# Routing attention and an ELU layer on one core: masks ahead of the scores in the ramp, weight conversion finished and weight sums made one block earlier

## The chip, the cores and the metric

The kernel runs on one core of a Trainium2 chip. The metric is the device time of one execution in microseconds (us). The kernel before the change takes 1039.99 us, the median of three runs (1039.98 to 1040.48). Engines carry the names of the profile: PE is the matrix engine, PEld its weight loads, DVE the vector engine, ACT the scalar engine, POOL the GpSimd engine, SP the queue that issues the transfers. "L252" is line 252 of the kernel before.

## What is computed

Attention in which a query sees only keys of its own cluster (the cluster is the nearest of 16 centroids, for queries and keys alike), and behind it a two-layer network with an ELU between the layers.

```python
# q, k, v: (4, 8, 768, 64) float32;  centroids: (8, 16, 64)
q_assign = argmax(q_n @ c_n.T);  k_assign = argmax(k_n @ c_n.T)
mask   = q_assign[:, :, :, None] == k_assign[:, :, None, :]
scores = where(mask, q @ k.T / 8, -1e9)
attn   = exp(scores - max) / sum(exp(scores - max))
x      = (attn @ v) -> (3072, 512)
# w_in: (512, 2048), w_out: (2048, 512): both arrive as float64
h = x @ w_in
g = where(h > 0, h, exp(min(h, 0)) - 1)
out = g @ w_out
```

The two weights are products of a float32 array and a float64 scalar, and so arrive as float64. [...]the kernel turns the 64-bit words into float32 by itself.

## The kernel before

The work is cut into 48 **blocks**: 4 batches, 3 thirds of 256 queries, 4 pairs of heads. Block n does the scores of block n and, one iteration later, the product with the values (`values(n)`). Seven blocks behind (`LAG = 7`) follows the network of a third, spread over four blocks: two blocks of `hidden` (the first layer) and two of `outer` (the second layer, seven half-size products in the manner of Strassen, which need sums and differences of the parts of `w_out`). The first seven blocks have no network beside them; they are called the ramp here. In the ramp the weights are converted, in 34 steps for 32 pieces of 128x512:

```python
def weight_steps():
    for n in range(len(pieces) + 2):
        if n > 1:          # finish piece n-2, then its buffer is free: ask for a later piece
            stt(ex, w[:, :, 1], 0x80000000, ex, bitwise_and, bitwise_or)     # DVE, L249
            stt(to, w[:, :, 0], 2.0**-32, to.bitcast(U32), mult, add)        # DVE, L252
            stt(to, to, 2.0**-20, ex.bitcast(F32), mult, mult)               # DVE, L255
            ask()                                                            # transfer on SP, L238
        if n < len(pieces):  # start piece n
            tensor_scalar(pieces[n][0], high, 0xFFFFF, 1 << 20, ...)         # DVE, L263
            tensor_scalar(e, high, 0x7FF00000, None, bitwise_and)            # DVE, L271
        if 0 <= n - 1 < len(pieces):
            activation(exps[n-1], exps[n-1], Relu, scale=8.0, bias=off)      # ACT, L274
        yield
def weigh(n): ...            # runs n of these steps
def sum_weights(half):       # e_, f_, g_, h_: quarters of w_out
    nc.vector.tensor_tensor(t1, f_, e_, op=subtract)     # DVE,  L304
    nc.gpsimd.tensor_tensor(f_, h_, f_, op=subtract)     # POOL, L305
    nc.vector.tensor_tensor(t2, h_, t1, op=subtract)     # DVE,  L306
    nc.vector.tensor_tensor(t4, g_, t2, op=subtract)     # DVE,  L307
```

The clusters become one-hot rows (`hot`), and a masked score is a second small matmul that adds `qm` times `hot`:

```python
def assign(b, j, at, size):          # j = 0: queries, in two halves of 384 (HS)
    ...                              # j = 1: keys, in batch 0 in three of 256 (QS)
    for e in range(2):
        if size == QS: nc.scalar.copy(h[64-at:128-at, 1, cols], h[at:at+64, 0, cols])    # ACT, L388
        else:   nc.vector.tensor_copy(h[64-at:128-at, 1, cols], h[at:at+64, 0, cols])    # DVE, L390
def masks(n):                        # qm of block n, two tiles in turn
    for e in range(2): nc.scalar.activation(qm[n][rows], hot[...], Identity, scale=m, ...)   # ACT, L401
def scores(n):                       # block 0 has a longer form
    for u in range(3):
        s = banks()                                  # one of three PSUM tiles of two banks
        ...                                          # PE: plain L425, mask L437
        nc.scalar.activation(p, s, Exp, scale=SCALE) # ACT, L448
        if n < LAG + 3: weigh(1)
def values(n):
    d = banks()
    ...                              # PE: p times v into o_bank L506; sums of p into d L495
    nc.scalar.activation(r, d, Ln)                    # ACT, L524
    nc.scalar.activation(e, d, Copy, accum_out=...)   # ACT, L525
    nc.scalar.activation(x, o_bank, Copy, scale=-1.0) # ACT, L526
    nc.scalar.activation(r, r, Exp, scale=-1.0)       # ACT, L527
    nc.vector.tensor_tensor(e, e, r, op=mult)         # DVE, L528
    nc.vector.scalar_tensor_tensor(r, e, -2.0, r, ...)# DVE, L529
    nc.gpsimd.tensor_tensor(x, x, r, op=mult)         # POOL, L532
def hidden(b, third, n):             # a quarter of the first layer
    h = banks(); ...                 # PE L547; ACT exp L557; POOL clip L558
    finish()                         # the elu of the quarter before: DVE L564, L566 or L568
def outer(b, third):                 # first .. fourth in one block, fifth .. seventh in the next
    first:  o_bank <- a, e_ ; ACT L608; DVE L609     second: f_bank <- b, g_ ; DVE L614, L615
    third_: o_bank <- c, f_ (written by L305)        fourth: f_bank <- d, t4 (written by L307); DVE L624
```

All products of `outer` have line L577. The order in which the blocks call all this:

```python
for n in range(len(blocks) + LAG):
    if n > 0: values(n - 1)
    ...                                        # loads of the next batch in blocks 5, 6, 9, 10; of v
    scores(n)
    masks(n + 1)
    if n >= LAG + 3: sums(n)
    turn(...)                                  # blocks 8 to 11: q and k of the next batch, DVE L319
    main = groups[n - LAG] if n >= LAG else []
    if n == LAG + 2:
        weigh(100)
        for half in range(2): sum_weights(half)
    for m, step in enumerate(main):            # hidden, or first .. fourth, or fifth .. seventh
        step()
        if n < LAG + 2: weigh(1)
```

Of the kernel before, what the change touches and what calls it, by code (L numbers as in the profile page):

```python
# [60 lines left out]
def main_path(ctx, tc, c, q, k, v, centroids, moe_w_in, moe_w_out, out):  # L61
# [8 lines left out]
    QS = S // NQ  # L70
# [38 lines left out]
    def load(name, i):  # L109
        b, pr = pairs[i]  # L110
        src = {"q": q, "k": k, "v": v}[name]
        if (name, i) in staged:
            t = first[:, ts(staged[name, i], 2 * NT * D)]
        elif name == "v":
            t = loads.tile([P, 2 * NT * D], F32, name="v_raw", tag="v", bufs=2)
        else:
            t = loads.tile([P, 2 * NT * D], F32, name=f"{name}_raw", tag="raw", bufs=4)
        if name == "v" or name == "q" and b == 0:
            t = t.rearrange("p (h t d) -> p h t d", h=2, t=NT)
            nc.sync.dma_start(  # L120
                t.rearrange("p h t d -> p h (t d)"),
                src[b, 2 * pr : 2 * pr + 2].rearrange("h (p t) d -> p h (t d)", t=NT),
            )
        elif b == 0:
            t = t.rearrange("p (t h d) -> p t h d", t=NT, h=2)
            for e in range(2):
                nc.sync.dma_start(
                    t[:, :, e], src[b, 2 * pr + e].rearrange("(p t) d -> p t d", t=NT)
                )
        else:  # L130

            for e in range(2):
                for g in range(2):
                    at = 64 * e + 32 * g
                    nc.sync.dma_start(
                        t[at : at + 32].rearrange("p (t a d) -> p t a d", t=NT, d=32),
                        src[b, 2 * pr + e, :, 32 * g : 32 * g + 32].rearrange(
                            "(a p t) d -> p t a d", a=4, t=NT
                        ),
                    )  # L140
        raw[name, i] = t
# [142 lines left out]
    def weigh(n):  # L284
        for _ in range(n):
            next(rest, None)
# [7 lines left out]
    def w_parts():  # L294
        e_, f_ = w_out[:, : FC // 2, :QS], w_out[:, : FC // 2, QS:]
        g_, h_ = w_out[:, FC // 2 :, :QS], w_out[:, FC // 2 :, QS:]
        return e_, f_, g_, h_

    def sum_weights(half):

        of = slice(half * FC // 4, (half + 1) * FC // 4)
        e_, f_, g_, h_ = (x[:, of] for x in w_parts())
        t1, t2, t4 = (w_sum[:, n, of] for n in range(3))
        nc.vector.tensor_tensor(t1, f_, e_, op=Alu.subtract)  # L304
        nc.gpsimd.tensor_tensor(f_, h_, f_, op=Alu.subtract)  # L305
        nc.vector.tensor_tensor(t2, h_, t1, op=Alu.subtract)  # L306
        nc.vector.tensor_tensor(t4, g_, t2, op=Alu.subtract)  # L307
# [38 lines left out]
    def similar(b, j, at, size):  # L346

        if at == 0:
            sim[b, j] = route.tile([P, S], F32, name="sim", tag="sim", bufs=1)
        ps = banks()[:, 0]  # L350
        cols = slice(at, at + size)
        for pr in range(NPR):
            nc.tensor.matmul(  # L353
                ps[32 * pr : 32 * pr + 32, :size],
                lhsT=cT[:, 32 * pr : 32 * pr + 32],
                rhs=T[b * NPR + pr, j][:, cols],
                start=True,
                stop=True,
            )
        return lambda: nc.vector.transpose(sim[b, j][:, cols], ps[:, :size])  # L360

    def assign(b, j, at, size):
        if at == 0:
            hot[b, j] = route.tile([P, 2, S], BF16, name="hot", tag=f"hot{j}", bufs=1 + j)
        cols = slice(at, at + size)
        n = size // NC
        s = sim[b, j][:, cols].rearrange("p (n c) -> p n c", c=NC)
        top = route.tile([P, HS // NC], F32, name="top", tag="top", bufs=1)[:, :n]
        oh = route.tile([P, HS], BF16, name="oh", tag="oh", bufs=1)[:, :size]
        nc.vector.tensor_reduce(top, s, axis=Axis.X, op=Alu.max)  # L370
        at = counted.setdefault(size, [])
        at.append(len(at) + (0 if size == HS else 4 * B - 2))
        at = at[-1]
        nc.vector.scalar_tensor_tensor(
            oh.rearrange("p (n c) -> p n c", c=NC),
            s,
            1.0,
            top.unsqueeze(2).to_broadcast([P, n, NC]),
            op0=Alu.mult,
            op1=Alu.is_equal,  # L380
            accum_out=count[:, at : at + 1],
        )
        h = hot[b, j]
        nc.vector.transpose(h[:, 0, cols], oh)  # L384
        for e in range(2):
            at = 64 * e
            if size == QS:
                nc.scalar.copy(h[64 - at : 128 - at, 1, cols], h[at : at + 64, 0, cols])  # L388
            else:
                nc.vector.tensor_copy(h[64 - at : 128 - at, 1, cols], h[at : at + 64, 0, cols])  # L390

    def side(pr, e):
        return int(pr // 2 != e)

    def masks(n):
        b, third, pr = blocks[n]
        qm[n] = route.tile([P, QS], BF16, name="qm", tag="qm", bufs=2)
        for e in range(2):
            rows = slice(64 * e, 64 * e + 64)
            m = big[rows, pr % 2 : pr % 2 + 1]  # L400
            nc.scalar.activation(  # L401
                qm[n][rows],
                hot[b, 0][rows, side(pr, e), ts(third, QS)],
                Act.Identity,
                scale=m,
                bias=minus[rows, pr % 2 : pr % 2 + 1],
            )


    LAG = 7  # L410
# [3 lines left out]
    blocks = [(b, third, pr) for b in range(B) for third in range(NQ) for pr in range(NPR)]  # L414
# [66 lines left out]
    def sums(n):  # L481
        to = osum[n] = work.tile([P, 2, 2 * QS], F32, name="psum", tag="psum", bufs=1)
        nc.vector.tensor_tensor(to, pu[n, 0], pu[n, 1], op=Alu.add)  # L483
        nc.vector.tensor_tensor(to, to, pu[n, 2], op=Alu.add)  # L484
        nc.vector.tensor_tensor(to[:, :, :QS], to[:, :, :QS], to[:, :, QS:], op=Alu.add)
# [174 lines left out]
    NB = NQ * NPR  # L660
# [3 lines left out]
    def load_v(n):  # L664
        b, third, pr = blocks[n]
        if n not in seen:
            seen.add(n)
            load("v", b * NPR + pr)
            raw["v", n] = raw.pop(("v", b * NPR + pr))
# [30 lines left out]
    for half in range(2):  # L700
        assign(0, 0, half * HS, HS)
    masks(0)

    for n in range(len(blocks) + LAG):
        b, at = n // NB, n % NB
        ahead = b + 1 < B
        if n <= len(blocks) and n > 0:
            values(n - 1)
        if ahead:
            for pr in {5: [0], 6: [1], 9: [2], 10: [3]}.get(at, []):  # L710
                load("q", (b + 1) * NPR + pr)
                load("k", (b + 1) * NPR + pr)
        if n + 1 < len(blocks):
            load_v(n + 1)
        if n < len(blocks):
            scores(n)
        if n + 1 < len(blocks) and at + 1 < NB:
            masks(n + 1)
        if n < len(blocks):
            if n >= LAG + 3:  # L720
                sums(n)
            if ahead and at in turns:
                for j in range(2):
                    turn((b + 1) * NPR + turns[at], j)
        beside = []
        if ahead and at + 1 == NB:
            beside.append(None)
            for j in range(2):
                beside.append(
                    lambda b=b, j=j: [similar(b + 1, j, half * HS, HS)() for half in range(2)]  # L730
                )
                beside.append(
                    lambda b=b, j=j: [assign(b + 1, j, half * HS, HS) for half in range(2)]
                )
            beside.append(lambda n=n: masks(n + 1))
        main = groups[n - LAG] if n >= LAG else []
        if n == LAG + 2:
            weigh(100)
            for half in range(2):
                sum_weights(half)  # L740
        done = 0
        for m, step in enumerate(main):
            step()
            upto = len(beside) * (m + 1) // len(main)
            for other in beside[done:upto]:
                if other:
                    other()
            done = upto
            if n < LAG + 2:
                weigh(1)  # L750
        for other in beside[done:]:
            if other:
                other()
        if n == len(blocks) + 1:
            verdict()

# [253 lines left out]
```

## Time and profile before

| | PE | PEld | DVE | ACT | POOL |
|---|---|---|---|---|---|
| busy, us of a span of 1038.0 | 1008.0 | 781.2 | 478.0 | 350.9 | 112.2 |
| share | 97% | 75% | 46% | 34% | 11% |

By stages, in us:

| stage | PE busy | DVE busy | ACT busy | granted PE clock |
|---|---|---|---|---|
| 0 to 26 | 17.39 | 19.28 | 14.26 | 1.00 |
| 26 to 52 | 24.02 | 17.39 | 17.21 | 0.93 |
| 52 to 78 | 24.22 | 23.13 | 19.43 | 1.00 |
| 78 to 104 | 24.37 | 23.97 | 17.73 | 1.00 |
| 104 to 130 | 25.80 | 21.45 | 13.11 | 1.00 |
| 130 to 156 | 21.69 | 25.62 | 9.02 | 0.96 |
| 156 to 182 | 24.11 | 13.44 | 5.79 | 0.78 |
| 312 to 1038 | 717.00 | 276.29 | 213.78 | 1.00 |

The table of stages is read as follows. In the last row PE is busy in 99 of 100 us. The stages with free PE time lie ahead of 182 us: block 0 ends near 34 us, the ramp near 98 us, and the first `outer` of the network begins at 144 us. The granted clock is the share of its full rate at which PE was allowed to run.

### The profile page before, as it was taken

The page shows a single profiled execution, that of the slowest core. Times are in us where ns is not written, and L with a number is a line of the kernel's source. Part 1 is how long each engine was busy: PE and PEld are TensorE (multiplying, and loading weights), DVE is VectorE, ACT ScalarE, POOL GpSimd, SP SyncE. Part 2 cuts the span into 40 slices and gives each one's busy share as a digit, 9 for nine tenths or more (in the row PEclk, how much of TensorE's full clock was granted, in tenths as well). Part 3 has the DMA queues.
Part 4 walks back from the last instruction along what each step waited for, and adds up shares of the span by engine and source line. Part 5 has one row for each costly group of instructions (what it writes and reads, how often), then busy time and mean ns, then how long its engine had stood idle before and what let it go on. Part 6 is the DMA issues. An engine that isn't in the chain of part 4 may idle for free.

```text
span 1038.0 us, 15007 instructions
## 1 busy us (share of the span) xinstructions
PE 1008.0 (97%) x6331; PEld 781.2 (75%) x6331; DVE 478.0 (46%) x775; ACT 350.9 (34%) x605; POOL 112.2 (11%) x129
## 2 busy tenths in 40 slices
PE   6999989999999999999999999999999999999997
PEld 4556766777777777778778778777877887788886
DVE  7689895463333334474234236365324423432121
ACT  5676532233332432333243243224223323421010
POOL 0001121110110110111011011011011011011010
PEclk9999997999999999999999999999999999999999
DMA  9738131100122113100122112201011010000000
GB/s 293 275 118 242 59 67 25 37 16 18 49 46 47 51 37 56 52 16 16 39 51 53 36 32 49 53 27 31 16 36 32 16 36 17 30 21 1 21 1 24
DMA packets 103962, 55.60 MB, mean 54 GB/s; under 512 B 83408, under 2 KB 96720, under 8 KB 103888
## 3 DMA queue, kind: packets, MB, share of 16 engines
q1 hardware_dynamic: 103888, 54.57, 19.2%
q8 instruction: 52, 0.85, 0.3%
q14 instruction: 22, 0.18, 0.0%
HBM read 48.27 MB, written 6.29 MB: 53 GB/s over the span
## 4 chain that ended last, share of the span: by engine, by line
PE 84%; DVE 10%; ACT 4%; issue 1%; POOL 0%; DMA 0%; DVEq 0%; ACTq 0%
PE banks L547 31%; PE f_bank L577 16%; PE o_bank L577 12%; PE o_bank L506 10%; PE banks L425 9%; PE banks L495 2%; PE banks L437 2%; DVE ex L249 1%; ACT p L448 1%; DVE w_in L252 1%; DVE w_out L252 1%; PE banks L353 1%; DVE w_in L255 1%; ACT e L525 1%; DVE ex L271 1%
## 5 line engine op out<-in xcount | busy, mean ns | idle before, releaser
L547 PE MATMUL banks<-xT,w_in 128*128 128x256 f32 x1536 | 338.4, 381 | 0.4 <-ACT p L448 0.2
L547 PEld LDWEIGHTS banks<-xT,w_in 128*128 128x128 f32 x1536 | 289.8, 190 | 48.0 <-issue 3.9
L425 PE MATMUL banks<-qT,kT 64*128 64x256 f32 x1152 | 167.2, 389 | 2.1 <-ACT e L525 0.8
L506 PE MATMUL o_bank<-p,v_raw 128*64 128x256 f32 x1152 | 144.6, 386 | 3.7 <-ACT p L448 3.7
L448 ACT ACTIVATE p<-banks 128x1024 f32<-128x1024 f32 x144 | 144.6, 1019 | 6.2 <-PE banks L437 4.2
L557 ACT ACTIVATE gT<-banks 128x1024 f32<-128x1024 f32 x48 | 49.1, 1023 | 279.1 <-PE banks L547 279.0
L564 DVE SCALAR_TENSOR_TENSOR gT<-gT,banks 128x1024 f32<-128x1024 f32 x48 | 58.4, 1217 | 156.4 <-POOL gT L558 156.3
L425 PEld LDWEIGHTS banks<-qT,kT 64*128 64x128 f32 x1152 | 87.7, 187 | 54.6 <-issue 11.1
L506 PEld LDWEIGHTS o_bank<-p,v_raw 128*64 128x64 f32 x1152 | 78.3, 137 | 57.3 <-issue 16.8
L524 ACT ACTIVATE r<-banks 128x256 f32<-128x256 f32 x48 | 18.4, 383 | 235.0 <-PE banks L495 234.9
L577 PE MATMUL o_bank<-w_out,gT 128*128 128x256 f32 x384 | 91.8, 393 | 6.2 <-POOL w_out L305 6.2
L528 DVE TENSOR_TENSOR e<-e,r 128x256 f32<-128x256 f32 x48 | 20.4, 425 | 161.0 <-ACT r L527 160.8
L577 PEld LDWEIGHTS o_bank<-w_out,gT 128*128 128x128 f32 x384 | 74.1, 196 | 20.6 <-POOL w_out L305 7.3
L558 POOL TENSOR_SCALAR gT<-gT 128x1024 f32<-128x1024 f32 x48 | 50.0, 1042 | 343.8 <-ACT gT L557 343.8
L577 PE MATMUL f_bank<-w_out,gT 128*128 128x256 f32 x384 | 86.8, 379 | 0.0
L532 POOL TENSOR_TENSOR xT<-xT,r 128x256 f32<-128x256 f32 x48 | 37.8, 788 | 448.4 <-DVE r L529 448.4
L437 PE MATMUL banks<-qm,hot 64*128 64x256 bf16 x576 | 81.3, 269 | 4.1 <-DVE hot L384 2.2
L577 PEld LDWEIGHTS f_bank<-w_out,gT 128*128 128x128 f32 x384 | 73.0, 190 | 9.9
L483 DVE TENSOR_TENSOR psum<-p 128x1024 f32<-128x1024 f32 x38 | 46.8, 1233 | 36.1 <-ACT p L448 36.1
L401 ACT ACTIVATE qm<-hot,minus,big 64x256 bf16<-64x256 bf16 x96 | 56.6, 590 | 1.1
L484 DVE TENSOR_TENSOR psum<-psum,p 128x1024 f32<-128x1024 f32 x38 | 46.6, 1226 | 5.9 <-ACT p L448 2.6
L577 PE MATMUL f_bank<-w_sum,g_sum 128*128 128x256 f32 x192 | 44.6, 386 | 0.6 <-DVE part L624 0.6
(111 smaller groups left out, 810.4 us busy)
## 6 DMA issues: line engine op xcount, KB each, us to landing
v_raw<-in_v_dram SPq DMA_DIRECT2D x48, 384.0 KB, 3.2
w_sum<-in_moe_w_out_dram SPq DMA_DIRECT2D x12, 512.0 KB, 4.4
out_dram<-o_sb SPq DMA_DIRECT2D x24, 256.0 KB, 2.1
q_raw<-in_q_dram SPq DMA_DIRECT2D x48, 96.0 KB, 3.2
k_raw<-in_k_dram SPq DMA_DIRECT2D x48, 96.0 KB, 2.9
w_sum<-in_moe_w_in_dram SPq DMA_DIRECT2D x8, 512.0 KB, 7.6
w_out<-in_moe_w_in_dram SPq DMA_DIRECT2D x8, 512.0 KB, 10.9
w_out<-in_moe_w_out_dram SPq DMA_DIRECT2D x4, 512.0 KB, 4.1
```

Source lines behind the costliest of these rows:

```text
L401: nc.scalar.activation(qm[n][rows], hot[b, 0][rows, side(pr, e), ts(third, QS)], Act.Identity, scale=m, bias=minus[rows, pr % 2 : pr % 2 + 1],
L425: nc.tensor.matmul(s[:, e, ts(kt % 2, QS)], lhsT=T[i, 1][rows, ts(kt, P)], rhs=T[i, 0][rows, cols], start=n > 0 or kt % 2 == 0, stop=False ...
L437: nc.tensor.matmul(s[:, e, ts(kt % 2, QS)], lhsT=hot[b, 1][rows, side(pr, e), ts(kt, P)], rhs=qm[n][rows], start=False, stop=True, skip_gr ...
L448: nc.scalar.activation(p, s, Act.Exp, scale=SCALE)
L483: nc.vector.tensor_tensor(to, pu[n, 0], pu[n, 1], op=Alu.add)
L484: nc.vector.tensor_tensor(to, to, pu[n, 2], op=Alu.add)
L506: nc.tensor.matmul(o_bank[64 * e : 64 * e + 64, :QS], lhsT=raw["v", n][:, e, kt], rhs=p[:, e, ts(m, QS)], start=(kt == 0), stop=(kt == NT ...
L547: nc.tensor.matmul(hf[:, f], lhsT=w_in[:, ch, ts(4 * n + f, P)], rhs=xT[b, third][:, ch], start=(ch == 0 and f % 2 == 0), stop=(ch == KC - 1),
L557: nc.scalar.activation(t, hf, Act.Exp)
L558: nc.gpsimd.tensor_scalar(t, t, 1.0, 0.0, op0=Alu.min, op1=Alu.max)
L564: nc.vector.scalar_tensor_tensor(t, t, -1.0, hf, op0=Alu.add, op1=Alu.max)
L577: nc.tensor.matmul(to[:, :QS], lhsT=left[:, f], rhs=right[:, f], start=(f == 0), stop=(f == FC // 2 - 1),)
```

## The change

Four things are moved, and no arithmetic is added or taken away. The copies of the queries' one-hot rows of batch 0 go from DVE to ACT. In blocks 1 to 9 the masks of the next block are issued ahead of the scores of this block, and so stand ahead of its exponentials in ACT's queue. Three conversion steps are run behind block 0, and in block 7 two steps follow each `hidden` instead of one. So all 34 steps are issued by the scores of block 8, and `sum_weights` runs at the end of block 8 instead of in block 9, ahead of the first products of `outer`. The aim is to use idle time of DVE in block 0, to shorten the wait between a block's last conversion step and its next one, and to have the sums of the weights ready when `outer` first wants them.

```diff
@@ assign
-            if size == QS:
+            if b == 0:
                 nc.scalar.copy(h[64 - at : 128 - at, 1, cols], h[at : at + 64, 0, cols])
@@ the loop over blocks
+        early = 0 < n < LAG + 3
+        more = n + 1 < len(blocks) and at + 1 < NB
+        if more and early:
+            masks(n + 1)
         if n < len(blocks):
             scores(n)
-        if n + 1 < len(blocks) and at + 1 < NB:
+        if more and not early:
             masks(n + 1)
+        if n == 0:
+            weigh(3)
...
-        if n == LAG + 2:
-            weigh(100)
-            for half in range(2):
-                sum_weights(half)
         done = 0
         for m, step in enumerate(main):
             step()
...
             if n < LAG + 2:
-                weigh(1)
+                weigh(2 if n == LAG else 1)
         for other in beside[done:]:
             if other:
                 other()
+        if n == LAG + 1:
+            weigh(100)
+            for half in range(2):
+                sum_weights(half)
```

## The prediction

> **What bounds the kernel now.** I read first the page's slices (the span in 40 equal parts of 26 us; digits are tenths of busy time, PEclk tenths of the full clock):
>
> ```profile
> PE   6999989999999999999999999999999999999997
> ...
> DVE  7689895463333334474234236365324423432121
> ...
> PEclk9999997999999999999999999999999999999999
> ```
>
> From the eighth slice (182 us) PE is full, so the time is the PE work plus what PE loses ahead of 182 us. DVE is nearly full in slices 3 to 6 only, and slice 7 has a low clock. Next the waits of DVE and of PE within the first 200 us (sum, times, longest):
>
> ```profile
> DVE e L528 <- ACT r L527: 26.3, 10, 6.7
> ...
> PE o_bank L577 <- POOL w_out L305: 6.2, 2, 4.3
> ...
> PE o_bank L506 <- ACT p L448: 3.7, 6, 0.7
> ```
>
> Two places lose time: the ramp, where PE waits a little in every block, and block 9, where PE waits for the sums of the weights. The chain of waits shows what paces a ramp block (start, us, what):
>
> ```profile
> 42.86 0.72 ACT ex L274
> 43.59 0.37 ACT qm L401
> ...
> 44.72 0.38 ACT r L524
> ...
> 46.20 0.44 DVE e L528
> ```
>
> The chain goes from a conversion on ACT (L274) through the two masks (L401) and the normaliser (L524 to L527) to DVE (L528), and from there through DVE's conversions. L528 begins at 46.20, 56.29, ... 96.65: a period of 10.08 us. In each DVE idles 0.77 us, and works 9.31.
>
> In DVE's timeline the end of block 0 shows a larger hole, behind the L271 that starts at 29.09 (the bracket is the idle time before, and what ended it):
>
> ```profile
> 36.20 0.43 DVE L528 TENSOR_TENSOR e<-e,r 128x256 f32<-128x256 f32 x1 [6.69 <-ACT r L527]
> ```
>
> and the timelines of DVE and PE in block 9 read
>
> ```profile
> 151.04 1.18 DVE L304 TENSOR_TENSOR w_sum<-w_out 128x1024 f32<-128x1024 f32 x1
> 152.25 1.22 DVE L306 TENSOR_TENSOR w_sum<-w_out,w_sum 128x1024 f32<-128x1024 f32 x1
> 153.51 3.25 DVE L307 TENSOR_TENSOR w_sum<-w_out,w_sum 128x1024 f32<-128x1024 f32 x1
> ```
>
> ```profile
> 144.24 3.72 PE L577 MATMUL o_bank<-w_out,gT 128*128 128x256 f32 x16
> 147.80 3.62 PE L577 MATMUL f_bank<-w_out,gT 128*128 128x256 f32 x16
> 155.73 3.78 PE L577 MATMUL o_bank<-w_out,gT 128*128 128x256 f32 x8 [4.31 <-POOL w_out L305]
> 161.40 3.78 PE L577 MATMUL o_bank<-w_out,gT 128*128 128x256 f32 x8 [1.89 <-POOL w_out L305]
> ```
>
> The third product stops twice for POOL, and its 8 records take as long as 16 did at 144.24: half the clock. The fourth, at 164.97, takes 4.90 us instead of 3.62.
>
> **What the Trainium skill says.** "TensorE: Matmul & The Clock Gate", section "What's actually happening": after an idle window of about 3.4 us PE falls to half rate, and needs about as long of busy time to come back. The trace agrees: after the idle 4.31 us the matmuls are half as fast, and are slow into the fourth product. The same page, section "Architectural detail: the array is 16× 32×32, not 1× 128×128": ACT and DVE are strict first-in first-out. So a mask issued after a conversion waits for it, as in the chain above. "SBUF — State Buffer", section "Who interferes with whom": DVE instructions with two SBUF inputs contend with POOL instructions that read SBUF. The trace agrees: L307 takes 3.25 us beside POOL's L305 (3.38), the same shape in L306 1.22. "Perfetto Trace Analysis", section "Optimizing Scalar/DVE Operations": work can go from a full DVE to ACT. In block 0, ACT idles 2.83 us ahead of its first key copy at 21.61.
>
> **The change part by part.**
>
> *Copies to ACT.* DVE loses two pairs of 64x384 copies, 0.55 and 0.44 us: about 1.0. ACT gains four; its own 64x384 copies (L342) take 0.96 a pair, so about 1.9 us more, into its idle 2.83. The first mask matmul (21.64) should come about 0.6 earlier and the last exponential of block 0 (27.69) about 1.0 earlier.
>
> *Three steps behind block 0.* From one L263 to the next (39.47 to 42.07) a step takes 2.60 us of DVE; three take 7.8. The hole of 6.69 plus the 1.0 saved is 7.7. So DVE becomes continuous here, and block 0's L528 stays at about 36.1. Gain at this point: nothing. These steps pay later, in block 9.
>
> *Masks ahead.* The two masks (43.49 to 44.70, 1.2 us) leave the stretch between the last conversion and L524. They then lie between L527 and the next exponential. New limits of a ramp block: DVE's work, 9.31. Or the loop DVE step, ACT conversion (0.7), third exponential (1.0), third part of the values on PE (1.8), L524 to L527 (1.5), L528/L529 and the next step (4.0): about 9.1 with the gaps. Or PE: values and row sums 12 groups of 0.433 (from one start to the next at full clock), 5.2, and scores 3.46 (34.60 to 38.06): 8.7. DVE is the longest. Six periods, L528 of block 0 to that of block 6, fall from 60.45 to 55.9: gain 4.6. The first exponential ends 2.1 us behind L528 instead of 0.9; the first `hidden` needs its PSUM tile and starts at L528 + 2.2 instead of + 1.46 (98.11 - 96.65). Net at the start of `hidden`: 3.9, at about 94.2.
>
> *Two steps per `hidden` in block 7.* Two more steps, 5.2 us, into a hole of 4.27 (before 118.99). With POOL's clips in the way L528 comes about 20.8 behind the start of `hidden`; before 20.88. Gain nothing, loss nothing.
>
> *Masks ahead in block 8.* Here one PSUM tile is held by the second `hidden`, whose ELU comes only in block 8. Before, PE's third score unit waited for the first exponential (0.3 us, 119.92) and the third `hidden` for the second (0.17 us, 121.44). Both are now pushed by 1.2 us of masks: loss 1.3.
>
> *Sums in block 8.* The last `hidden` ended at 135.46. ACT's exponential, POOL's clip and the ELU (2.1 + 1.9) end 4.1 us later; then `sum_weights` takes what it took before, 151.04 to 162.4, 11.3 us. So counted from the end of `hidden`, X: both L305 are done at X + 4.1 + 5.65 + 1.2 + 3.4 = X + 14.4, all sums at X + 15.4. PE wants `f_` (third product) at X + 15.8 and `t4` (fourth) at X + 19.3: the waits vanish, with 1.4 us to spare. DVE comes to L614, which frees f_bank for the fourth product, after L528/L529 (0.9), two transposes (1.8), L609 (1.2) and itself (0.4): X + 19.7 to 20. Loss 0.6. Before, 144.24 to 169.81 were 25.57 us for four products of 3.49: 11.6 lost. Gain 11.0.
>
> The sum: 3.9 - 1.3 + 11.0 = 13.6 us. All later PE work is full and moves up as it is: 1040.0 - 13.6 = 1026.4 us.
>
> **The rivals.**
>
> *The wait only moves.* If the sums on DVE start late (two contended L307, the steps of block 8, the transposes), the third product stops for L305 again. For: the slack is only 1.4 us, and DVE is nearly full from 130 to 156 us (25.62 of 26). Against: five of eight conversion steps of blocks 8 and 9 are gone from that stretch, 5 x 2.6 = 13 us. A wait of some 2 us without the half clock: 1029; long enough for the half clock: 1032 or more.
>
> *The masks take from the exponentials what they give to the normaliser.* PE takes up the values about 3.6 us after the scores began, and the first exponential then ends about when PE wants it. For: PE already waits for L448 0.7 us a block. Against: that wait is for the third exponential, which hangs on the conversion and not on the masks. If it happens, the ramp gains 0 to 1: 1030.
>
> *A transfer takes over.* The three steps behind block 0 put three weight transfers ahead of the next v transfer in SP's queue, which then leaves at about 36.5 instead of 34.28, and must land by 46.5. v took 3.2 us to landing in the median, 9.9 for the one at 26.88. Two us of wait once: 1028.4.
>
> *Better than the sum.* Block 0 ends with half clock (27.6 to 31.05, where 16 records took 3.4 us instead of 1.7). With shorter waits there the clock may stay up: 1.7 us more, 1024.7.
>
> **Range and chances.** The block 9 term is the surest, as it is read as a hole in PE; the ramp term depends on DVE having no new gaps (between 0.5 and 4.6 us), block 0 on the clock (up to 1.7 either way). I take 1022.5 to 1030.5. 2% would be 20.8 us, below 1019.2; all holes and half clocks I have named come to 11.6 + 4.6 + 1.7 = 17.9. So faster by over 2% gets 0.04, within 2% 0.94, slower by over 2% 0.02.
>
> **What would show it.** Right: L528 in the ramp every 9.3 us, with no idle time of DVE before it; DVE without a hole from 26 to 36 us; no wait for L305 and a full clock in the slice of block 9; four products from start to values in 14 to 15 us. Wrong in the ramp: a period near 10, with PE waiting for L448 at the first unit of the values. Wrong in block 8: no wait of PE for L448 ahead of the third `hidden`, which would add the 1.3 us. Wrong in block 9: PE waiting for L305 or L614 for more than 1 us. The prediction falls if PE after 170 us shows new holes, for it takes the rest as unchanged.

## The result, and the profile after

The changed kernel takes 1026.03 us (median of four runs, 1025.86 to 1026.78), against 1039.99 before (four runs by then, 1038.40 to 1040.48): a ratio of 0.987, with a 95% interval of 0.9853 to 0.9887. Predicted were 1026.4 us. The profiled spans are 1024.7 and 1038.0 us.

The page's slices of the changed kernel (25.6 us each, digits in tenths):

```profile
PE   6999999999999999999999999999999999999997
...
DVE  7999972753244244473334344375224324423131
...
PEclk9999999999999999999999999999999999999999
```

The dip of PE and of its clock in slices 6 and 7 is gone. DVE is now full from slice 2 to slice 5, so its hole at the end of block 0 is filled. The waits of DVE within the first 200 us (sum, times, longest) begin with

```profile
DVE e L528 <- ACT r L527: 10.7, 2, 6.4
```

Before these were ten waits with a sum of 26.3 us. Of the two that are left none lies in the ramp (they begin at 163.45 and 180.64). The waits of PE in the same time:

```profile
PE o_bank L506 <- ACT p L448: 1.9, 6, 0.8
...
PE banks L425 <- ACT p L448: 1.2, 1, 1.2
...
PE f_bank L577 <- DVE o_sb L614: 0.2, 1, 0.2
```

The wait for POOL's L305 is no longer among them. A new one, L425 for L448, is 1.2 us long. In the chain of waits of one ramp block (start, us, what)

```profile
46.08 0.37 DVE e L528
...
54.98 0.34 DVE ex L271
55.32 0.36 DVE e L528
```

everything between these lines is DVE: ACT has left the chain, and each L528 follows the last conversion instruction without a pause. But ACT is only just ahead. In its timeline of the same block

```profile
53.89 0.39 ACT L524 ACTIVATE r<-banks 128x256 f32<-128x256 f32 x1 [0.41 <-PE banks L495]
...
54.79 0.42 ACT L527 ACTIVATE r<-r 128x256 f32<-128x256 f32 x1
```

the normaliser (L524 to L527), which waits for PE, ends at 55.21, and DVE's timeline has L528 start at 55.25. So DVE's own work and the loop from DVE through ACT's conversion, the third exponential, PE's values and the normaliser back to L528 end within 0.04 us of each other. This trace does not tell which of the two sets the period of 9.23 us.

In DVE's timeline there is no pause at the end of block 0 either:

```profile
36.52 0.42 DVE L271 TENSOR_SCALAR ex<-w_sum 128x512 uint32<-128x512 uint32 x1
36.85 0.42 DVE L528 TENSOR_TENSOR e<-e,r 128x256 f32<-128x256 f32 x1
```

The sums of the weights in DVE's timeline, and the first four products of `outer` in PE's:

```profile
137.30 1.22 DVE L304 TENSOR_TENSOR w_sum<-w_out 128x1024 f32<-128x1024 f32 x1
138.55 1.22 DVE L306 TENSOR_TENSOR w_sum<-w_out,w_sum 128x1024 f32<-128x1024 f32 x1
139.81 3.26 DVE L307 TENSOR_TENSOR w_sum<-w_out,w_sum 128x1024 f32<-128x1024 f32 x1
```

```profile
141.94 3.72 PE L577 MATMUL o_bank<-w_out,gT 128*128 128x256 f32 x16
145.49 3.62 PE L577 MATMUL f_bank<-w_out,gT 128*128 128x256 f32 x16
148.95 3.62 PE L577 MATMUL o_bank<-w_out,gT 128*128 128x256 f32 x16
152.81 3.72 PE L577 MATMUL f_bank<-w_sum,gT 128*128 128x256 f32 x16 [0.24 <-DVE o_sb L614]
```

The sums cost DVE what they cost before, but they start 4.6 us ahead of the first product instead of 6.8 behind it. All four products run at full clock. What the change costs stands in PE's timeline of block 8:

```profile
117.48 0.70 PE L425 MATMUL banks<-qT,kT 64*128 64x256 f32 x4 [1.25 <-ACT p L448]
...
119.14 14.08 PE L547 MATMUL banks<-xT,w_in 128*128 128x256 f32 x64 [0.30 <-ACT p L448]
```

The third score unit and the third `hidden` wait for exponentials that now stand behind the masks.

Behind this the two programs move alike: from the first product of the first second half of `outer` (178.59 before, 165.25 after) to the last product of all (1029.18, 1015.82) it is 850.59 and 850.57 us. So the gain lies ahead of that point, and five numbers of each trace tell where. They are used for all runs below: the L528 of block 0, the ramp's period (mean of six), the start of the first `hidden`, from there to the third `hidden`, and from the first product of `outer` to the fifth, which holds the hole of block 9.

| run | L528, block 0 | period | first hidden | to third hidden | first to fifth product | time, us |
|---|---|---|---|---|---|---|
| before | 36.20 | 10.08 | 98.11 | 23.33 | 34.35 | 1039.99 |
| after | 36.85 | 9.23 | 94.47 | 24.67 | 23.31 | 1026.03 |
| e1, masks late | 36.88 | 10.08 | 98.79 | 23.66 | 23.32 | 1029.89 |
| e2, masks to 7 | 36.48 | 9.23 | 94.11 | 23.31 | 23.31 | 1025.38 |
| e3, copies on DVE | 37.71 | 9.29 | 95.66 | 24.66 | 23.31 | 1027.88 |
| e4, sums in block 9 | 36.94 | 9.23 | 94.59 | 24.66 | 26.01 | 1029.62 |
| e5, no steps in block 0 | 34.67 | 9.26 | 92.47 | 24.66 | 25.86 | 1027.60 |
| e6, no sign | 36.29 | 9.02 | 92.64 | 24.65 | 23.31 | 1024.16 |
| e7, masks only | 36.56 | 9.24 | 94.22 | 24.67 | 32.07 | 1034.89 |
| e8, two steps | 35.84 | 9.23 | 93.47 | 23.31 | 23.32 | 1023.42 |
| e9, sums only | 37.26 | 10.08 | 99.19 | 23.66 | 23.31 | 1030.60 |
| e10, after again | 36.22 | 9.24 | 93.88 | 24.66 | 23.31 | 1026.85 |
| e11, masks to 6, two steps | 35.11 | 9.24 | 92.45 | 23.33 | 23.32 | 1023.32 |
| e12, PE filled | 33.64 | 9.35 | 91.64 | 23.33 | 23.31 | 1023.08 |

The times are medians of four runs each. The same changed kernel took 1026.03 and 1026.85 us on two occasions, and its L528 of block 0 came at 36.85 and 36.22. The runs were made in three groups (e1 to e4, e5 to e8, e9 to e12), each on another chip, where the kernel before took 1039.68, 1039.83 and 1039.51 us. So a difference below 1 us between times of different groups is not read as an effect; the stages are, though each stage is from one trace.

### The profile page after: what moved, and what is told of

It reads as the page before. It is cut to its first block, busy times and chain, and to the rows that moved or that the text cites. A ratio compares the mean times of both kernels' runs of the same rounds, so it can differ in the third digit from the quotient of the medians.

```text
span 1024.7 us, 15010 instructions
## 1 busy us (share of the span) xinstructions
PE 1001.1 (98%) x6331; PEld 778.4 (76%) x6331; DVE 474.8 (46%) x771; ACT 354.1 (35%) x609; POOL 112.5 (11%) x129
## 4 chain that ended last, share of the span: by engine, by line
PE 81%; DVE 12%; ACT 3%; issue 2%; DMA 1%; POOL 0%; SPq 0%; DVEq 0%; POOLq 0%; ACTq 0%
PE banks L547 30%; PE f_bank L577 16%; PE o_bank L577 12%; PE o_bank L506 10%; PE banks L425 9%; PE banks L437 2%; PE banks L495 2%; DVE ex L249 2%; DVE w_in L252 1%; DVE w_in L255 1%; DVE w_out L252 1%; ACT p L448 1%; DVE ex L271 1%; PE banks L353 1%; DVE w_out L255 1%
## 5 line engine op out<-in xcount | busy, mean ns | idle before, releaser
L425 PE MATMUL banks<-qT,kT 64*128 64x256 f32 x1152 | 166.0, 388 | 3.3 <-ACT p L448 1.2
L448 ACT ACTIVATE p<-banks 128x1024 f32<-128x1024 f32 x144 | 144.5, 1020 | 6.4 <-PE banks L437 4.2
L425 PEld LDWEIGHTS banks<-qT,kT 64*128 64x128 f32 x1152 | 88.0, 187 | 53.0 <-PE o_bank L506 10.0
L524 ACT ACTIVATE r<-banks 128x256 f32<-128x256 f32 x48 | 18.4, 384 | 232.9 <-PE banks L495 232.9
L577 PE MATMUL o_bank<-w_out,gT 128*128 128x256 f32 x384 | 87.8, 382 | 0.0
L528 DVE TENSOR_TENSOR e<-e,r 128x256 f32<-128x256 f32 x48 | 20.4, 424 | 145.4 <-ACT r L527 145.2
L532 POOL TENSOR_TENSOR xT<-xT,r 128x256 f32<-128x256 f32 x48 | 37.4, 779 | 435.5 <-DVE r L529 380.8
L483 DVE TENSOR_TENSOR psum<-p 128x1024 f32<-128x1024 f32 x38 | 46.6, 1226 | 36.1 <-ACT p L448 36.1
```

Of the source, the lines that this page charges most:

```text
L425: nc.tensor.matmul(s[:, e, ts(kt % 2, QS)], lhsT=T[i, 1][rows, ts(kt, P)], rhs=T[i, 0][rows, cols], start=n > 0 or kt % 2 == 0, stop=False ...
L448: nc.scalar.activation(p, s, Act.Exp, scale=SCALE)
L577: nc.tensor.matmul(to[:, :QS], lhsT=left[:, f], rhs=right[:, f], start=(f == 0), stop=(f == FC // 2 - 1),)
```

## The experiments

**e1: masks behind the scores.** The changed kernel with

```diff
-        early = 0 < n < LAG + 3
+        early = False
```

> The changed kernel with the masks behind the scores again, in all blocks. My theory: the masks' 1.2 us go back into the stretch between the last conversion on ACT and the normaliser, so L528 in the ramp comes every 10.0 to 10.1 us instead of 9.23, with DVE idle 0.8 us before each: +5.1. The first hidden then starts 1.46 instead of 2.24 us behind L528: -0.8; block 8 loses its waits for the exponentials: -1.3. Sum +3.0, 1029.0 us. Rival: the ramp is paced by DVE's work alone and the gain came from the steps moved ahead; then the period stays 9.23 and the time is 1024.7 to 1026 us.

Measured 1029.89 us, where 1029.0 was expected. The period is 10.08 again, to the hundredth that of before, although the steps are moved and the copies are on ACT. So it is the order of the masks that makes the difference between 10.08 and 9.23, and not the moved steps: the rival is out. The third `hidden` comes 1.0 us sooner behind the first, where 1.3 was expected.

**e2: masks early in blocks 1 to 7.**

```diff
-        early = 0 < n < LAG + 3
+        early = 0 < n < LAG + 1
```

> The changed kernel, with the masks ahead of the scores in blocks 1 to 7 only, not in 8 and 9. My theory: the 1.25 us that PE's third score unit of block 8 waits for the first exponential are due to the masks of block 9 standing ahead of it; without them that wait falls to about 0.3 and the third hidden starts 23.3 instead of 24.67 us behind the first: 1024.7 us. Rival: the wait comes from the conversions between the exponentials on ACT; then nothing changes, 1026.0 us.

Measured 1025.38 us, between the theory and the rival, so the time alone does not decide. The trace does: from the first `hidden` to the third it is 23.31 us instead of 24.67, the expected 1.35. The wait of 1.25 us of the third score unit is no longer there. The masks of block 9 are what kept it waiting, not the conversions, which stand between the exponentials here too.

**e3: copies on DVE again.**

```diff
-            if b == 0:
+            if size == QS:
                 nc.scalar.copy(h[64 - at : 128 - at, 1, cols], h[at : at + 64, 0, cols])
```

> The changed kernel with the queries' one-hot copies of batch 0 on DVE again. My theory: DVE works without a hole from block 0's first finished piece to the end of the ramp, so whatever delays that start delays all: the first conversion on ACT (25.60) comes 0.8 to 1.0 us later, and so does L528 of block 0: 1026.8 to 1027.0 us. Rival: the copies lie beside other work; no change, 1026.0 us.

Measured 1027.88 us, a little above the theory. L528 of block 0 comes at 37.71, 0.86 us later than in the changed kernel's first trace and 1.49 later than in its second; the first conversion on ACT starts at 26.25 instead of 25.60. The copies are on the path, as expected. The exact size stays between 0.9 and 1.5 us, as L528 of the changed kernel itself differs by 0.63 between its two traces. The longer mean period, 9.29, is one block: there L528 (56.41) waits 0.23 us for ACT's L527, so the loop through ACT and PE can end last.

**e4: sums in block 9.** The `weigh(100)` and the `sum_weights` go back behind the scores and transposes of block 9; the steps stay where the change put them.

```diff
+        if n == LAG + 2:
+            weigh(100)
+            for half in range(2):
+                sum_weights(half)
         done = 0
...
-        if n == LAG + 1:
-            weigh(100)
-            for half in range(2):
-                sum_weights(half)
```

> The changed kernel with the sums of the weights back in block 9, all conversion still done by block 8. My theory: most of the 11 us of block 9 came from the conversion being through; the sums then start about 142.7, behind L528 and the transposes; the third product waits about 2.4 us for the second L305 and the fourth starts about 2.9 us later than now, with no half clock: 1028.9 us. Rival: the place of the sums is what counts; then the waits of before return with the half clock, +11: 1037 us.

Measured 1029.62 us. In PE's timeline the third product is split once:

```profile
149.06 1.89 PE L577 MATMUL o_bank<-w_out,gT 128*128 128x256 f32 x8
153.07 1.99 PE L577 MATMUL o_bank<-w_out,gT 128*128 128x256 f32 x8 [2.12 <-POOL w_out L305]
```

It waits 2.12 us and goes on at full clock; with L614 it is 2.70 us in all (26.01 against 23.31), 2.9 expected. So with the conversion through, 8.3 of the 11 us of block 9 are there already, and the place of the sums adds 2.7. The sums begin 0.64 us behind the first product here (142.69 and 142.05), and 6.80 behind it in the kernel before.

**e5: no steps behind block 0.**

```diff
-        if n == 0:
-            weigh(3)
```

> The changed kernel without the three conversion steps behind block 0; they then fall to the last hidden of block 8. My theory: block 0's L528 waits for ACT and not for DVE and comes 1.3 us earlier, and the ramp with it: -1.3. In block 8 three more steps lie on DVE ahead of the sums, which start about 2 us later; the third product still finds its parts, but L614 comes about 2 us later and the fourth product waits: +1.9. Sum +0.6: 1026.7 us. Rival: the three steps are what keeps the sums off PE's path; without them the third product waits again: 1029 us or more.

Measured 1027.60 us (1027.31 to 1030.52), where 1026.7 was expected. The bill is as expected in kind. Block 0's L528 waits for ACT, and comes at 34.67, 1.6 to 2.2 us earlier. In block 8 the last three steps lie ahead of the sums, and PE's timeline has

```profile
153.35 3.72 PE L577 MATMUL f_bank<-w_sum,gT 128*128 128x256 f32 x16 [2.80 <-DVE o_sb L614]
```

a wait for L614 of 2.80 instead of 0.24 us, and none for L305. So the three steps cost 1.6 to 2.2 us in block 0 and give 2.55 in block 9 (25.86 against 23.31): they are worth little.

**e6: no sign.** The changed kernel leaving out L249, so that the weights have no sign and the output is another; all else is the same work.

```diff
-                nc.vector.scalar_tensor_tensor(
-                    ex, w[:, :, 1], 0x80000000, ex, op0=Alu.bitwise_and, op1=Alu.bitwise_or
-                )
```

> The changed kernel, leaving out one of the five DVE instructions of each conversion step, L249, which puts the sign in (so the weights lose their signs). My theory: DVE's 9.23 us of work pace the ramp; with 3 x 0.60 us less PE becomes the limit, at 8.7 to 8.8 us a block: 6 x 0.45 = 2.7, and block 0's L528 1.3 earlier: 1022 us. Rival: ACT's chain of conversion, exponential and normaliser paces the ramp; then only block 0 gains, 1024.7 us.

Measured 1024.16 us, a miss against the 1022 of my theory. The trace says why (lines have numbers three lower here). In DVE's timeline

```profile
54.33 0.42 DVE L525 TENSOR_TENSOR e<-e,r 128x256 f32<-128x256 f32 x1 [1.46 <-ACT r L524]
```

DVE idles 1.46 us a block, so it is not the bound here. The period falls only to 9.02 us. PE's timeline shows it with scores from 43.77, values from 47.46 behind a wait of 0.16 us for the first exponential, and the next scores at 52.79: PE is the limit at 9.02, of which 8.86 are its own work, and not at the 8.7 that I had taken from starts of groups without the change-overs. The gain is 6 x 0.21 = 1.3 us in place of 2.7. In block 0 the half clock lasted longer in this run (a mean clock of 0.50 from 28 to 32 us, 0.61 in the changed kernel's first trace), and L528 came at 36.29. The run does not show whether DVE's work or the loop through ACT and PE held the 9.23: without L249 DVE has three instructions less to do in a block, and the loop is one instruction of 0.60 us shorter too.

**e7: masks only.** The kernel before with the masks ahead of the scores in blocks 1 to 9, as in the change, and nothing else of it.

```diff
+        early = 0 < n < LAG + 3
+        more = n + 1 < len(blocks) and at + 1 < NB
+        if more and early:
+            masks(n + 1)
         if n < len(blocks):
             scores(n)
-        if n + 1 < len(blocks) and at + 1 < NB:
+        if more and not early:
             masks(n + 1)
```

> The kernel before, with the masks ahead of the scores in blocks 1 to 9 as the only change. My theory: the ramp's period falls to 9.3 us, -4.9 over six blocks; the first hidden starts 0.75 later behind L528; block 8 loses 1.3; block 9 keeps its waits for L305: in all -2.8, 1037.2 us. Rival: without the other parts the masks bring nothing, 1040 us.

Measured 1034.89 us, 2.3 better than expected. The stages up to block 9 are as expected: period 9.24, first product at 141.69, 2.55 us earlier than before. The rest is in block 9, in PE's timeline:

```profile
152.53 1.99 PE L577 MATMUL o_bank<-w_out,gT 128*128 128x256 f32 x8 [3.67 <-POOL w_out L305]
158.20 3.38 PE L577 MATMUL o_bank<-w_out,gT 128*128 128x256 f32 x8 [3.68 <-POOL w_out L305]
161.42 3.62 PE L577 MATMUL f_bank<-w_sum,gT 128*128 128x256 f32 x16
```

PE waits longer than before (7.35 us instead of 6.20), but after the first wait the clock is still full, and only the second half of the product is slow. From the first product to the fifth it is 2.28 us less: the waits are 1.15 us longer, but fewer records ran at half clock (the fourth product takes 3.62 us, before 4.90). That is nearly all of the 2.3.

**e8: two steps behind block 0, masks to block 7.** In the changed kernel:

```diff
-        early = 0 < n < LAG + 3
+        early = 0 < n < LAG + 1
...
-            weigh(3)
+            weigh(2)
```

> The changed kernel with two steps behind block 0 instead of three, and the masks ahead in blocks 1 to 7 only. My theory: -1.3 from block 8 (as in the run with masks to 7), and with two steps DVE is done before the normaliser of block 0, whose L528 comes 1.3 us earlier; the one step that is left falls into a hole of DVE in block 8: 1023.4 us. Rival: what block 0 gives is lost to the sums in block 8: 1024.7 us.

Measured 1023.42 us, as expected in sum. The block 8 part is there (23.31 us to the third `hidden`), and the wait for L614 stays 0.25 us. L528 of block 0 waits for ACT again and comes at 35.84, which is 1.01 and 0.38 us earlier than in the changed kernel's two traces, not 1.3; this trace is of the slowest of the four runs (1024.41). So that the sum fits so closely is in part luck.

**e9: steps and sums only.** The kernel before with the three steps behind block 0, two per `hidden` in block 7, and the sums at the end of block 8.

```diff
+        if n == 0:
+            weigh(3)
...
-        if n == LAG + 2:
...
-                weigh(1)
+                weigh(2 if n == LAG else 1)
...
+        if n == LAG + 1:
```

> The kernel before with only the steps moved (three behind block 0, two per hidden in block 7) and the sums in block 8; masks and copies as before. My theory: block 9 is whole, 14.5 instead of 25.6 us for the four products, -11.0; the ramp keeps its 10.08 us; block 0's L528 comes 1.3 us later, as DVE has the copies and three more steps there: in all -9.7, 1030.2 us. Rival: the block 9 gain needs the faster ramp too; then 1033 us or more.

Measured 1030.60 us, 8.9 less than the 1039.51 of before in the same group. The block 9 hole is gone whole (23.31) with the ramp at 10.08, so this gain does not need the faster ramp; e7 shows that the ramp's does not need the sums. -8.9 here and -4.9 in e7 make 13.8, and the change gave 14.0, but that is no proof that the two add up: the 2.3 us that e7 gained in block 9 stand in both, and the copies on ACT (0.9 to 1.5 us by e3) in neither.

**e10: the changed kernel again**, unchanged.

> The changed kernel once more, unchanged, beside the three others on the same chip: 1026.0 us, within 0.7.

Measured 1026.85 us (1026.12 to 1027.37), just outside the 1025.3 to 1026.7 that were expected.

**e11: masks to block 6, two steps.**

```diff
-        early = 0 < n < LAG + 3
+        early = 0 < n < LAG
...
-            weigh(3)
+            weigh(2)
```

> The changed kernel with two steps behind block 0 and the masks ahead in blocks 1 to 6 only. Masks of block 7 no longer stand ahead of the exponential that frees the PSUM tile of the first hidden: 0.3 us less than with masks to 7 and two steps (1023.4): 1023.1 us. Rival: the first hidden waits for POOL's last xT and not for the tile; then 1023.4 us.

Measured 1023.32 us, against 1023.42 of e8 in another group: the times can't tell 0.3 us. The traces can. The first `hidden` starts 1.92 us behind L528 (92.45 and 90.53) instead of 2.24, without a wait, while POOL's last xT was still at work in POOL's timeline:

```profile
91.69 1.08 POOL L532 TENSOR_TENSOR xT<-xT,r 128x256 f32<-128x256 f32 x1 [8.24 <-DVE r L529]
```

It ends at 92.77, behind that start. So the wait that the changed kernel's trace puts down to POOL's L532 (0.25 us at 94.47) was for the PSUM tile, and the exponential that frees it ended at 94.33.

**e12: PE filled in block 0.** The kernel of e11, with six more matmuls into `f_bank` that nobody reads:

```diff
                 for m in range(2):
                     mask(units[u], 2 * u + m)
+                for _ in range(2 * (u + 1) if u < 2 else 0):
+                    nc.tensor.matmul(f_bank[:, :QS], lhsT=T[i, 1][0:64, ts(0, P)],
+                                     rhs=T[i, 0][0:64, cols], start=True, stop=True)
                 exponentials(units[u], u)
```

> The kernel of the run with masks to 6 and two steps, with six more small matmuls in block 0 whose results nobody reads, in the gaps where PE waits for masks and exponentials. Theory that the half clock behind block 0 (16 to 22 records at half speed) comes from those gaps: the clock stays full, the values of block 0 end 1.8 to 2.2 us earlier, L528 with them, 1021.3 us. Rival: the clock follows something else or has its own beat; then nothing, or up to 0.5 us more, 1023.1 to 1023.6 us.

Measured 1023.08 us (1021.89 to 1023.47) against 1023.32 (1022.58 to 1024.00) of e11: no difference that these runs resolve. But the first half of the theory holds. The stages of e11 and of this run, with PE's busy time first (behind the length) and the granted clock behind POOL's:

```profile
24.00:28.00 4.00, 1.99 (x13) 0.86 (x12) 2.90 (x8) 3.60 (x6) 0.00 (x0) 0.78 1.03 413
28.00:32.00 4.00, 4.00 (x32) 2.43 (x30) 3.77 (x9) 3.02 (x6) 0.00 (x0) 0.79 1.03 411
```

```profile
24.00:28.00 4.00, 3.46 (x26) 2.25 (x26) 2.98 (x7) 3.85 (x6) 0.00 (x0) 1.00 1.02 408
28.00:32.00 4.00, 4.00 (x40) 2.46 (x37) 3.96 (x9) 2.96 (x6) 0.00 (x0) 1.00 1.03 410
```

With PE busy 3.46 of 4 us the clock stays full (the mean clock of the whole span is 0.999 to 1.000 in the four runs, 0.997 to 0.998 in those of e11), and L528 of block 0 comes at 33.64, 1.47 earlier than in e11. Then a transfer takes over, in PE's timeline of block 1 (lines from L470 on are eight higher):

```profile
36.65 0.65 PE L514 MATMUL o_bank<-p,v_raw 128*64 128x256 f32 x4 [1.27 <-DMA v_raw<-in_v_dram]
```

The v of block 1 leaves SP at 26.67, behind 14 weight transfers, and PE now wants it before it is there. In DVE's timeline the next L528 then waits 0.63 us for ACT, and the first `hidden` is 0.8 us earlier, no more. An earlier place for this v in SP's queue was not tried.

## Why the prediction was right

**Block 0.** Predicted: copies moved to ACT, DVE without a hole, L528 where it was. It came at 36.85 and 36.22 in two traces, before at 36.20, predicted 36.1. The hole is gone: from 26.36 on, DVE's timeline of the first trace has no pause up to L528. e3 shows the copies on the path, e5 that the three steps take the room the copies made, and more.

**The ramp.** Predicted 4.6 us from 0.77 us of idle time a block; measured 60.45 - 55.38 = 5.07. What paced the ramp before was named rightly: e1 brings the old period back with the masks, e7 takes it away with nothing else. What paces it now is half shown: DVE has no idle time left, as predicted, but the loop that the prediction put at about 9.1 us closes at 9.23 as well, and no run here parts the two. DVE's 9.31 us were 0.08 too long: I counted the last conversion instruction to its end, and the next begins 0.08 us ahead of that. The 8.7 for PE was the worst number of the working; e6 puts it at 8.86, and the period that PE can hold at 9.02. It was not in the sum, but it made the ramp look as if 0.6 us a block were left to gain, where there are 0.2.

**The first hidden.** Predicted 2.2 us behind L528, measured 2.24. The rival that the masks take from the exponentials all that they give to the normaliser did not come true: only block 1 waited 0.8 us for its first exponential (1.2 in e10), the later blocks 0.2 or less.

**Block 8.** Predicted a loss of 1.3 us, measured 24.67 - 23.33 = 1.34, and shown by e2 to come from the masks of block 9.

**Block 9.** Predicted 11.0 us, measured 34.35 - 23.31 = 11.04. The four products took 14.52 us (141.94 to 156.46), 0.56 more than four of 3.49, where 0.6 had been allowed; the trace puts 0.24 of it down to L614. e4 and e9 show that the waits vanish as the conversion is through and the sums are early, and that they do not need the faster ramp.

**The sum.** 13.6 us predicted, 13.96 by the medians, 13.3 by the spans. The terms of the two traces are -0.65 (block 0), 5.07 (ramp), -0.78 (first `hidden`), -1.34 and 11.04, together 13.34. The largest errors are the gain of 0.5 us too little in the ramp and the loss of 0.65 in block 0 that was not foreseen (0.02 in the trace of e10), and they partly cancel: so close a sum is in part luck. The transfer rival did not come true: in the changed kernel the v of block 2 left SP at 35.98 (predicted 36.5) and PE never waited for it. PE waited 0.31 us for a later v, at 85.30, and the period did not move. The half clock behind block 0 stayed too. In e12 the half clock goes, and a wait for a v comes.

The best version measured is that of e11 and e12, with a ratio to before of 0.9846 (0.9829 to 0.9862) and 0.9841 (0.9825 to 0.9858).

## What to carry to other kernels

On an engine with a first-in first-out queue, an instruction that is ready early should not be issued behind one that waits for another engine: here the masks behind the conversion cost 0.85 us in each ramp block. But look at each block what then stands behind it: the same order cost 1.3 us where PSUM tiles were short. When one engine has to prepare something in time, count its work up to the deadline: here five conversion steps of 2.60 us, about 13 us, left the stretch ahead of it, and with that 8.3 of the 11.0 us of block 9 were won; moving the sums gave 2.7.

## What the runs showed of the hardware that was not expected

The same kind of hole costs PE more or less, as its clock falls earlier or later. Before, a wait of 4.31 us was followed by half clock at once (8 records in 3.78 us); in e7 a wait of 3.67 us was not (1.99 us), and the next, of 3.68, was (3.38). The Trainium skill, "TensorE: Matmul & The Clock Gate", section "What's actually happening", says that the window of activity runs freely, and does not start anew with the kernel. This fits it, but does not show it: before the second wait of e7 PE had worked only 1.99 us since the first, and no run here measured the window. And one wait of that page's 3.4 us is not needed: behind block 0 of e11 the clock fell with no gap of more than 1.11 us, when PE was busy 1.99 of 4 us, and it stayed full when six matmuls without use made it 3.46.

Work on DVE beside POOL was slowed in some places and not in others. In the changed kernel POOL's L305 runs from 138.60 to 141.98. L306, which began 0.05 us ahead of it, took 1.22 us; L307, of the same shape, began 1.2 us into it and took 3.26. So the prediction's pair of L307 and L306 is not one with and one without POOL: both ran beside it. In the ramp the L252 behind each L528 took about 1.22 us beside POOL's L532 (at 47.50 in the changed kernel, with L532 from 47.12 to 48.17), and 0.68 or 0.69 in the other steps of the block. That is 0.54 us of the 9.23 of each block, in DVE's work and in the loop alike; moving it was not tried.
